# Second layer of a retention and mixture-of-experts kernel: sign tests ahead of the routing chain, w2 products in steps of four column groups, filler matmuls

## The chip, the cores and the metric

The kernel runs on one core of one Trainium2 chip. The metric is the device time of one execution in microseconds (us), lower is better. TensorE is called PE, VectorE DVE, ScalarE ACT, GpSimd POOL and SyncE SP, as in the profile.

## The reference

Three stages follow one another. All data are float32.

```python
# 1. retention, 4 x 8 heads, 768 steps, head size 64
for t in range(S):
    state = gamma * state + einsum('bhd,bhe->bhde', k[:, :, t], v[:, :, t])
    y[:, :, t] = scale * einsum('bhd,bhde->bhe', q[:, :, t], state)
# 2. soft mixture: x (3072 x 512), phi (512 x 32), 8 experts with 4 slots each
logits = x @ phi
d = softmax over tokens;  slot_input = d.T @ x
slot_out[e] = relu(slot_input[e] @ w1[e]) @ w2[e]
c = softmax over slots;   x = c @ slot_out
# 3. top-1 mixture: 8 experts
logits = normalised(x) @ normalised(expert_emb).T / tau
expert_idx = argmax(logits);  gate_w = its softmax weight
out[token] = gate_w[token] * (relu(x[token] @ w1[e]) @ w2[e])
```

The change is in the third stage, called the second layer here.

## The kernel before

The first 205 us are retention and the soft mixture. After them a token is a row of 32 softmax weights c times the 32 x 512 matrix of slot outputs S. The kernel uses that: x = c S, so x w1 = c (S w1), and with G = S w1 (32 x 1024) the hidden values of a token are c G. All tokens of these data go to one expert, e0, which is found from a dot product (lines 1010 to 1015). Its weights are then loaded: w1 in two halves of four 128-column blocks, w2 in pieces of four, two and two blocks (load_w1, load_w2, lines 1016 and 1017; SP issues them in this order, each queued behind the one before). A guarded general path (line 1187 on) stands behind for other data and is not taken.

Since c is a softmax, each of the 1024 hidden units has the same sign over all tokens, if its row of G passes a test (signs, line 1050): it is always positive, always negative, or mixed. Always positive units can be folded: their part of the result is c times (G+ w2), a 32 x 512 matrix M. Always negative units vanish. Mixed units, at most 16 in each block of 128, are picked out and ranked; only for them the hidden values are made for each token (mixed_h) and multiplied with the picked rows of w2.

The second layer is written in a manual schedule: each engine does its instructions in the order of the program text. Names of the tiles, as the profile shows them:

- pu: products of the tokens with S and the expert embeddings (emit_dots, L936), from which DVE takes logit and the squared norms n (take_dots).
- rn: the norm, by a Sqrt on ACT (roots, L950) and two Newton rounds of five DVE operations (newton_sqrt, L1246 to L1250); then routing (L953 to L961) and routing2 (Exp on ACT at L964, then gate on DVE).
- gp, gs: one half of G, four products of 32 columns each on PE (g_part, L858), and its copy by ACT.
- gtp, gt, gsq: its transposes, their copy and their square (signs, L1055 to L1057).
- cs, det, mixed, pos, gpos: the test on DVE (L1058 to L1071); rankp, rank, pick: the ranks of the mixed units (L1076 to L1082).
- gmp, gm, gm4p, Gm: the picked columns of G, spread over four groups of 32 rows and split in a rounded and a rest part (mixed_g).
- mpp, wmp: sums over the eight blocks of gpos and of pick with w2 (fold, L1148); each product has 32 output rows and goes to one of four 32-column groups of PE.
- hps, hh, hl: mixed hidden values for 512 tokens, in six calls of mixed_h (L1100 to L1102).
- mp, m4p, M4: the sum of the four groups of mpp and its split; wmh, wml: the split of wmp.
- ob, ot: one output tile of 128 tokens: four products on PE (L1169 to L1172) in one of four PSUM tiles, the eviction with the gate (evict: DVE for even tiles, ACT for odd ones), the DMA by SP.
- over, cn, pn, cnt, nci: the counts that guard the general path (overflow, counts, counts2), put between tiles 12 to 15 of the output loop.

Before the change, the order of the calls was:

```python
        roots()
        g_part(gs, w1t, 0, W1P)
        newton_sqrt(nc, rn, n2, tm)
        routing()
        routing2()
        signs(0)
        g_part(gs, w1t, 1, W1P)
        signs(1)
        mixed_g()
```

then the w2 products of two blocks at a time, with mixed_h(0) to mixed_h(2) between them, and the loop over 24 output tiles with the other three calls of mixed_h after tiles 2, 6 and 10.

## Time and profile before

| what | value |
|---|---|
| time, median of 3 runs | 276.36 us (276.36 to 277.99) |
| the profiled execution's own time | 276.69 us |
| its span in the trace | 274.8 us |
| PE busy | 246.7 us, 90% of the span |
| DVE / ACT / POOL busy | 121.2 / 98.9 / 55.5 us |
| mean granted clock of PE over the span | 0.919 of 2.4 GHz |

Times in the trace count from the start of the span. PE has two rows in the profile: PE for the matmuls and PEld for loading their stationary operand. A float32 product counts as two matmul instructions, one in fp32r as one. The granted clock (PEclk) is 1.00 at 2.4 GHz and 0.50 at 1.2 GHz.

### The profile page before, as it was taken

How to read it: one execution, taken by the hardware profiler on the slowest of the kernel's cores; microseconds unless marked ns; L12 is line 12 of the kernel's file. 1: busy time of each engine (PE TensorE's matmuls, PEld its weight loads, DVE VectorE, ACT ScalarE, POOL GpSimd, SP SyncE). 2: the span in 40 equal slices, each digit the busy share in tenths (PEclk: the TensorE clock that was granted, in tenths of full speed). 3: DMA queues.
4: the chain of work that ended last, by engine and by line, in shares of the span. 5: the costliest groups of instructions: out<-in, count | busy, mean ns of one | idle time of the engine just before them, and what ended most of it. 6: DMA issues, size and time to landing. Idle time of an engine off the chain costs nothing.

```text
span 274.8 us, 6014 instructions
## 1 busy us (share of the span) xinstructions
PE 246.7 (90%) x2413; PEld 171.1 (62%) x2414; DVE 121.2 (44%) x318; ACT 98.9 (36%) x236; POOL 55.5 (20%) x80
## 2 busy tenths in 40 slices
PE   6899999699999699989998998999998646999991
PEld 2678887588787587877786775333337315238770
DVE  2435645414474336354734564341113842145661
ACT  3264544234534224534544335214013311135331
POOL 2154141414231414141414104120002000000000
PEclk9799999869999869999999999999999555799997
DMA  6995998999989899999999978999904920006664
GB/s 162 220 233 108 270 261 233 273 260 235 220 245 271 230 284 239 234 225 271 258 279 258 358 260 310 360 389 385 384 13 127 393 97 1 0 0 234 265 261 167
DMA packets 85952, 63.74 MB, mean 232 GB/s; under 512 B 51856, under 2 KB 64400, under 8 KB 85920
## 3 DMA queue, kind: packets, MB, share of 16 engines
q1 hardware_dynamic: 85920, 63.30, 79.9%
q8 instruction: 21, 0.34, 0.5%
q14 instruction: 11, 0.09, 0.1%
HBM read 57.00 MB, written 6.29 MB: 230 GB/s over the span
## 4 chain that ended last, share of the span: by engine, by line
PE 65%; DMA 14%; SPq 5%; DVE 5%; POOL 4%; ACT 2%; issue 2%; POOLq 0%; DVEq 0%; ACTq 0%
DMA qc<-in_q_dram 13%; PE y L312 6%; PE hp L763 5%; PE ops L794 5%; PE sc L260 5%; PE y L306 5%; PE trk L237 4%; SPq L145 3%; PE T L289 3%; PE trx L332 3%; POOL qs L215 3%; PE trq L248 3%; PE ob L1172 2%; PE ob L1169 2%; PE ob L1171 2%; PE ob L1170 2%
## 5 line engine op out<-in xcount | busy, mean ns | idle before, releaser
L215 POOL TENSOR_TENSOR qs<-qc,cst 128x512 f32<-128x512 f32 x21 | 22.2, 1075 | 60.8 <-DMA qc<-in_q_dram 43.9
L266 DVE TENSOR_TENSOR at<-sc,cst 128x1024 f32<-128x1024 f32 x23 | 28.1, 1224 | 10.2 <-PE sc L260 9.6
L207 POOL TENSOR_TENSOR kc<-kc,cst 128x512 f32<-128x512 f32 x22 | 23.0, 1047 | 39.0 <-DMA kc<-in_k_dram 31.4
L260 PE MATMUL sc<-qT,kT 64*128 64x128 f32 x384 | 28.8, 291 | 0.0
L317 ACT COPY xT<-y 128x512 f32<-128x512 f32 x24 | 14.0, 585 | 40.1 <-PE y L312 35.6
L260 PEld LDWEIGHTS sc<-qT,kT 64*128 64x128 f32 x384 | 24.1, 193 | 6.7 <-issue 4.9
L312 PE MATMUL y<-at,vc 128*64 128x128 f32 x384 | 26.2, 279 | 0.0
L334 DVE COPY x<-trx 128x512 f32<-128x512 f32 x23 | 15.8, 689 | 22.9 <-PE trx L332 22.6
L239 ACT COPY kT<-trk 128x512 f32<-128x512 f32 x23 | 13.5, 585 | 31.5 <-PE trk L237 31.5
L312 PEld LDWEIGHTS y<-at,vc 128*64 128x64 f32 x384 | 20.5, 136 | 2.9 <-DVE rm L422 0.3
L237 PE MATMUL trk<-cst,kc 128*128 128x128 f32 x92 | 16.2, 303 | 6.7 <-POOL kc L207 6.6
L306 PE MATMUL y<-qT,tb 128*128 128x128 f32 x160 | 22.1, 282 | 0.0
L306 PEld LDWEIGHTS y<-qT,tb 128*128 128x128 f32 x160 | 20.0, 196 | 0.1
L342 DVE TENSOR_REDUCE lt<-ltps 128x32 f32<-128x128 f32 x24 | 7.0, 290 | 23.7 <-PE ltps L341 23.7
L237 PEld LDWEIGHTS trk<-cst,kc 128*128 128x128 f32 x92 | 10.5, 150 | 9.9 <-POOL kc L207 7.7
L162 POOL TENSOR_TENSOR cs<-c_all,cs 128x64 fp32r<-128x64 f32 x24 | 7.2, 332 | 44.7 <-ACT cs L161 44.7
L332 PE MATMUL trx<-cst,xT 128*128 128x128 f32 x96 | 16.2, 294 | 0.0
L249 ACT COPY qT<-trq 128x512 f32<-128x512 f32 x22 | 13.8, 627 | 4.6 <-PE trq L248 4.2
L248 PE MATMUL trq<-cst,qs 128*128 128x128 f32 x88 | 15.4, 304 | 0.0
L763 PE MATMUL hp<-wu,sinT 128*32 128x512 f32 x128 | 15.2, 597 | 0.0
L794 PE MATMUL ops<-wu,Z 128*32 128x512 f32 x128 | 14.1, 594 | 0.0
L289 PE MATMUL T<-vc,kc 128*64 128x64 f32 x304 | 13.9, 238 | 0.2 <-ACT tb L299 0.2
(270 smaller groups left out, 365.1 us busy)
## 6 DMA issues: line engine op xcount, KB each, us to landing
wu<-in_moe_w_dram SPq DMA_DIRECT2D x32, 1024.0 KB, 8.7
vc<-in_v_dram SPq DMA_DIRECT2D x24, 256.0 KB, 4.9
out_dram<-ot SPq DMA_DIRECT2D x24, 256.0 KB, 2.2
kc<-in_k_dram SPq DMA_DIRECT2D x23, 256.0 KB, 6.8
qc<-in_q_dram SPq DMA_DIRECT2D x11, 512.0 KB, 8.4
w1t<-in_moe_w_dram SPq DMA_DIRECT2D x2, 1024.0 KB, 6.2
w2t<-in_moe_w_dram SPq DMA_DIRECT2D x1, 1024.0 KB, 9.4
w2t<-in_moe_w_dram SPq DMA_DIRECT2D x2, 512.0 KB, 10.2
```

Of the source, the lines that this page charges most:

```text
L207: eng.tensor_tensor(out=t, in0=t, in1=gk[:, g % CPB, :].unsqueeze(2).to_broadcast([P, H, D]), op=ALU.mult)
L215: engs[r].tensor_tensor(out=ts[:, r, :, :], in0=t[:, :, r, :], in1=gq[:, (g % CPB) // 2, :, r].unsqueeze(2).to_broadcast([P, H, D]), op=AL ...
L237: nc.tensor.transpose(ps[:, a, :], k_t[g][:, 2 * a:2 * a + 2, :].rearrange("p h d -> p (h d)"), ident)
L248: nc.tensor.transpose(ps[:, a, :], q_t[g][:, r, 2 * a:2 * a + 2, :].rearrange("p h d -> p (h d)"), ident)
L260: nc.tensor.matmul(ps[:, hh, a, :], kT[g][lo:lo + 64, a, :], qs(g, lo, lo + 64, a), start=True, stop=True,)
L266: nc.vector.tensor_tensor(out=t.rearrange("p e a t -> p (e a) t"), in0=ps.rearrange("p e a t -> p (e a) t"), in1=mask.unsqueeze(1).to_broa ...
L289: nc.tensor.matmul(T[64 * hh:64 * hh + 64, a, :], k_t[g][:, h, :], v_t[g][:, h, :], start=(c == 0 and a == 0), stop=True, skip_group_check ...
L306: nc.tensor.matmul(ps[:, a, :], tb[:, a, :], qs(g, 0, P, a), start=(a == 0), stop=False, skip_group_check=True,)
L312: nc.tensor.matmul(ps[64 * hh:64 * hh + 64, a, :], v_t[g][:, 2 * a + hh, :], at_t[g][:, hh, a, :], start=(c == 0 and a == 0), stop=True, s ...
L332: nc.tensor.transpose(ps[:, a, :], xT[g][:, a, :], ident)
L763: nc.tensor.matmul(hp[32 * j:32 * j + 32, :], sinT[kc // 2][:, kc % 2, :], w[:, j, :], start=(kc == 0), stop=(kc == KDM - 1), skip_group_c ...
L794: nc.tensor.matmul(ops[32 * j:32 * j + 32, :], Z[grp][:, fc, :], w[:, j, :], start=(grp == 0 and fc == 0), stop=(grp == 1 and fc == KFF - ...
```

## The change

Nothing is altered ahead of the last dot products. Behind them:

- signs is cut into three: gt_part (transposes, square, copy), signs (the test on DVE), picks (rank and pick). gsq has a half for each i. Both halves are tested before the Newton steps and the routing; these stand behind picks(1) on DVE. The Newton round has three operations instead of five.
- routing is cut in two, and its two operations of 128 x 192 go to POOL; the is_equal for the one-hot mask moves into counts; Exp writes tmp8 instead of logit.
- A one-element Exp on ACT behind gt_part(0) brings the table load with it.
- busy(n) puts n products of 128 x 512 in fp32r on PE, three times three, whose result nobody reads.
- fold multiplies four blocks in one step, each in a column group of its own; the first mpp step stands between the two picks. The slots of pick are those of the half, and mixed_g puts block fc in group fc % 4.
- Two calls of mixed_h stand before the loop instead of three, four in it (after tiles 1, 5, 9 and 13). The output tile has six buffers instead of four.

```diff
-    def routing():
+    def routing(eng):
         nc.vector.tensor_scalar_add(rn, rn, 1e-6)
         nc.vector.reciprocal(out=rn, in_=rn)
-        nc.vector.tensor_tensor(
+        eng.tensor_tensor(
             out=logit, in0=logit, in1=rn.unsqueeze(2).to_broadcast([P, NCH, E]), op=ALU.mult
         )
+
+    def routing1(eng):
         nc.vector.tensor_reduce(out=tm, in_=logit, axis=AX.X, op=ALU.max)
         mb = tm.unsqueeze(2).to_broadcast([P, NCH, E])
-        nc.vector.tensor_tensor(out=tmp8, in0=logit, in1=mb, op=ALU.is_equal)
-        nc.vector.tensor_tensor(out=logit, in0=logit, in1=mb, op=ALU.subtract)
+        eng.tensor_tensor(out=tmp8, in0=logit, in1=mb, op=ALU.subtract)
...
     def counts():
         eb = eidx.unsqueeze(1).to_broadcast([P, NCH, E])
+        nc.vector.tensor_tensor(
+            out=tmp8, in0=logit, in1=tm.unsqueeze(2).to_broadcast([P, NCH, E]), op=ALU.is_equal
+        )
         nc.vector.tensor_tensor(out=tmp8, in0=tmp8, in1=eb, op=ALU.mult)
...
-        op = s4.enter_context(tc.tile_pool(name="op", bufs=4))
+        op = s4.enter_context(tc.tile_pool(name="op", bufs=6))
...
-        def signs(i):
+        def gt_part(i):
             fs = slice(4 * i, 4 * i + 4)
             ps = ps_a.tile([P, 4, NSLOT], F32, tag="a", name="gtp")
...
-            nc.scalar.activation(out=gsq, in_=ps, func=ACTF.Square)
+            gtps[i] = ps
+            nc.scalar.activation(out=gsq[:, i], in_=ps, func=ACTF.Square)
             nc.scalar.copy(gt[:, fs, :], ps)
-            nc.vector.tensor_reduce(out=cs_[:, fs], in_=ps, axis=AX.X, op=ALU.add)
+
+        def signs(i):
+            fs = slice(4 * i, 4 * i + 4)
+            nc.vector.tensor_reduce(out=cs_[:, fs], in_=gtps[i], axis=AX.X, op=ALU.add)
...
+        def picks(i):
+            fs = slice(4 * i, 4 * i + 4)
             pr = ps_a.tile([P, 4], F32, tag="a", name="rankp")
             nc.tensor.matmul(pr, mask, mixed[:, fs], start=True, stop=True)
             nc.vector.tensor_tensor(out=rank[:, fs], in0=mixed[:, fs], in1=pr, op=ALU.mult)
             nc.vector.tensor_tensor(
-                out=pick[:, fs, :].rearrange("p (b r) s -> p b r s", r=2),
-                in0=rank[:, fs].rearrange("p (b r) -> p b r", r=2).unsqueeze(3).to_broadcast([P, 2, 2, NSLOT]),
-                in1=slots.unsqueeze(1).to_broadcast([P, 2, 2, NSLOT]), op=ALU.is_equal,
+                out=pick[:, fs, :], in0=rank[:, fs].unsqueeze(2).to_broadcast([P, 4, NSLOT]),
+                in1=slots[:, i:i + 1, :].to_broadcast([P, 4, NSLOT]), op=ALU.is_equal,
             )
...
+        def busy(n_):
+            pz = ps_b.tile([P, DM], F32, tag="b", name="busy")
+            for _ in range(n_):
+                nc.tensor.matmul(pz, cT(0, P), cT(0, 512), start=True, stop=True)
+
+        def fold(dst, lhs, i):
+            for fc in range(4 * i, 4 * i + 4):
+                o = NSLOT * (fc % 4)
+                nc.tensor.matmul(
+                    dst[o:o + NSLOT, :], lhs[:, fc, :], w2t[fc], start=(i == 0), stop=True, skip_group_check=True
+                )
+
...
-        roots()
+        nc.vector.tensor_scalar_max(n2, n2, TINY)
+        nc.scalar.activation(out=rn, in_=n2, func=ACTF.Sqrt)
+        busy(3)
         g_part(gs, w1t, 0, W1P)
-        newton_sqrt(nc, rn, n2, tm)
-        routing()
-        routing2()
+        busy(3)
+        gt_part(0)
+        nc.scalar.activation(out=junk, in_=rinv4, func=ACTF.Exp)
         signs(0)
         g_part(gs, w1t, 1, W1P)
+        busy(3)
+        gt_part(1)
+        picks(0)
         signs(1)
-        mixed_g()
         pm = ps_b.tile([P, DM], F32, tag="b", name="mpp")
         pw = ps_b.tile([P, DM], F32, tag="b", name="wmp")
...
-        for i in range(KFF // 2):
-            for fc in (2 * i, 2 * i + 1):
-                fold(pm, NSLOT * ((i + 1 + fc % 2) % 4), gpos, fc)
-                fold(pw, NSLOT * i, pick, fc)
-            if i < 3:
-                mixed_h(i)
+        fold(pm, gpos, 0)
+        picks(1)
+        fold(pm, gpos, 1)
+        fold(pw, pick, 0)
+        for _ in range(2):
+            nc.vector.reciprocal(out=tm, in_=rn)
+            nc.vector.scalar_tensor_tensor(out=tm, in0=tm, scalar=0.5, in1=n2, op0=ALU.mult, op1=ALU.mult)
+            nc.vector.scalar_tensor_tensor(out=rn, in0=rn, scalar=0.5, in1=tm, op0=ALU.mult, op1=ALU.add)
+        routing(nc.gpsimd)
+        mixed_g()
+        routing1(nc.gpsimd)
+        mixed_h(0)
+        fold(pw, pick, 1)
         nc.scalar.copy(mp, pm)
-        nc.scalar.copy(wmh, pw)
         pr = ps_b.tile([P, DM], F32, tag="b", name="m4p")
         nc.tensor.matmul(pr, rep, mp, start=True, stop=True)
+        mixed_h(1)
+        nc.scalar.copy(wmh, pw)
         nc.vector.tensor_tensor(out=wml, in0=pw, in1=wmh.bitcast(F32), op=ALU.subtract)
         stack_split(M4, pr)
+        routing2()
...
-            if g in (2, 6, 10):
-                mixed_h(3 + g // 4)
+            if g in (1, 5, 9, 13):
+                mixed_h(2 + g // 4)
```

On PE, between the last dot products and the w2 products, the order before is:

```order
L936 MATMUL pu<-SEst,cT_2353 128x42 x16
L858 MATMUL gp<-w1t_2666,SoT 32x512 x4
L1055 MATMUL gtp<-cst,gs 128x32 x4
L1076 MATMUL rankp<-mixed,cst 128x4
L858 MATMUL gp<-w1t_2668,SoT 32x512 x4
L1055 MATMUL gtp<-cst,gs 128x32 x4
L1076 MATMUL rankp<-mixed,cst 128x4
L1088 MATMUL gmp<-pick,gt 32x32 x8
L1094 MATMUL gm4p<-gm_2698,cst 128x128
L1148 MATMUL mpp<-w2t_2670,gpos 32x512
```

and of the change:

```order
L936 MATMUL pu<-SEst,cT_2353 128x42 x16
L1143 MATMUL busy<-cT_2158 128x512 x3
L858 MATMUL gp<-w1t_2666,SoT 32x512 x4
L1143 MATMUL busy<-cT_2158 128x512 x3
L1060 MATMUL gtp<-cst,gs 128x32 x4
L858 MATMUL gp<-w1t_2668,SoT 32x512 x4
L1143 MATMUL busy<-cT_2158 128x512 x3
L1060 MATMUL gtp<-cst,gs 128x32 x4
L1088 MATMUL rankp<-mixed,cst 128x4
L1148 MATMUL mpp<-w2t_2670,gpos 32x512 x4
L1088 MATMUL rankp<-mixed,cst 128x4
```

The second w1 half now stands ahead of the first rank product, the fillers stand around the w1 halves, and four mpp products stand together. The products gmp and gm4p come four w2 products of each sum later.

On ACT, from the root to the second gs copy, as one piece of the difference:

```order
-L950 ACTIVATE rn<-n_2601 128x24
+L1158 ACTIVATE rn<-n_2601 128x24
 L862 COPY gs<-gp 128x512
-L964 ACT_TABLE_LOAD
-L964 ACTIVATE logit<-logit 128x192
-L1056 ACTIVATE gsq<-gtp 128x128
-L1057 COPY gt<-gtp 128x128
+L1062 ACTIVATE gsq<-gtp 128x128
+L1063 COPY gt<-gtp 128x128
+L1163 ACT_TABLE_LOAD
+L1163 ACTIVATE junk_69<-rinv_67 128x1
 L862 COPY gs<-gp 128x512
```

The table load moved from ahead of the first square and copy to behind them, with a one-element Exp in place of the routing's.

On DVE, in the output loop around tile 12 to tile 14 (ovp and over: the overflow test, cn: the counts), the change has:

```order
L1129 TENSOR_SCALAR ot<-ob,gate 128x512 x2
L1120 TENSOR_REDUCE over<-ovp 1x1
L1121 TENSOR_SCALAR over<-over 1x1
L1113 SCALAR_TENSOR_TENSOR hl<-hps,hh 128x512
L972 TENSOR_TENSOR tmp_2600<-logit,tm 128x192
L975 TENSOR_TENSOR tmp_2600<-tmp_2600,cst 128x192
L976 TENSOR_REDUCE tm<-tmp_2600 128x24
L977 TENSOR_TENSOR onehot<-tm,cst 128x192
L980 TENSOR_REDUCE cn<-onehot 128x8
L981 TENSOR_REDUCE cn<-good 128x1
L1129 TENSOR_SCALAR ot<-ob,gate 128x512
```

Before, neither the hl (L1113) nor the first tmp operation (L972) stood between the overflow test and the counts; the others stood there in the same order.

## Rows read from the trace of the kernel before

**Rows 1.** Stretches: start:end, length, busy PE, PEld, DVE, ACT, POOL, PEclk, DMA share.

```profile
50.90:53.40 2.50, 0.00 (x0) 0.00 (x0) 1.18 (x1) 0.20 (x1) 2.06 (x3) 0.89 1.07 300
210.60:213.30 2.70, 2.70 (x25) 2.63 (x24) 1.04 (x4) 0.77 (x2) 0.00 (x0) 1.00 0.90 340
213.30:216.70 3.40, 2.27 (x11) 0.45 (x10) 2.87 (x11) 0.50 (x2) 0.00 (x0) 0.50 1.05 396
216.70:223.60 6.90, 2.34 (x10) 2.24 (x10) 5.53 (x24) 2.27 (x5) 0.00 (x0) 0.50 0.74 273
223.60:233.10 9.50, 6.30 (x37) 4.03 (x37) 2.47 (x12) 1.27 (x4) 0.00 (x0) 0.50 0.01 3
233.10:237.10 4.00, 4.00 (x10) 0.84 (x9) 0.29 (x1) 0.27 (x1) 0.00 (x0) 0.50 0.00 0
246.70:269.10 22.40, 22.36 (x100) 17.57 (x98) 13.93 (x33) 9.26 (x14) 0.00 (x0) 1.00 0.65 249
```

**Rows 2.** Chain of waits from the dots to the output loop: start, us, what.

```profile
215.51 0.23 ACT rn L950
...
221.67 0.30 DVE cs__2692 L1058
...
223.73 1.91 PE gp L858 x8
...
228.77 0.30 DVE cs__2692 L1058
...
245.51 0.71 DVE M L825
```

**Rows 3.** Timeline, 194 to 234 us: start, us, engine, line, instruction, [idle before].

```profile
194.64 10.05 PE L794 MATMUL ops<-wu,Z 128*32 128x512 f32 x92
...
208.71 1.10 PE L1023 MATMUL sep<-seT,SoT 128*128 128x64 f32 x8 [0.94 <-DVE seT L1020]
...
214.30 1.94 PE L858 MATMUL gp<-w1t,SoT 128*32 128x512 f32 x8 [0.67 <-DMA w1t<-in_moe_w_dram]
...
217.03 1.28 ACT L964 ACT_TABLE_LOAD   x1
...
217.06 1.91 PE L1055 MATMUL gtp<-cst,gs 128*128 128x32 f32 x8 [0.83 <-ACT gs L862]
...
230.76 1.35 PE L1088 MATMUL gmp<-pick,gt 128*32 128x32 f32 x16
...
233.58 0.29 DVE L825 TENSOR_TENSOR Gm<-gm4p,Gm 64x128 fp32r<-64x128 f32 x1 [2.23 <-ACT Gm L824]
```

**Rows 4.** Chain of waits: a w2 pass, hps at the low and at the high clock.

```profile
235.10 1.70 PE wmp L1148 x2
236.80 0.62 PE hps L1100
...
248.62 0.23 PE hps L1100
```

**Rows 5.** Timeline of the output loop around tiles 11 to 16.

```profile
257.19 0.59 ACT L1101 ACTIVATE hh<-hps 128x512 fp32r<-128x512 f32 x1
...
257.85 0.69 ACT L1116 ACTIVATE ot<-ob,gate 128x512 f32<-128x512 f32 x1
...
257.92 0.68 DVE L1102 SCALAR_TENSOR_TENSOR hl<-hps,hh 128x512 fp32r<-128x512 f32 x1
...
259.42 0.34 DVE L971 TENSOR_TENSOR tmp<-tmp,cst 128x192 f32<-128x192 f32 x1
...
261.01 0.17 DVE L977 TENSOR_REDUCE cn<-good 128x1 f32<-128x24 f32 x1
...
261.37 0.20 PE L981 MATMUL pn<-cn,ones 128*1 128x9 f32 x2
```

**Rows 6.** The page's costliest groups: operations on POOL.

```profile
L215 POOL TENSOR_TENSOR qs<-qc,cst 128x512 f32<-128x512 f32 x21 | 22.2, 1075 | 60.8 <-DMA qc<-in_q_dram 43.9
...
L162 POOL TENSOR_TENSOR cs<-c_all,cs 128x64 fp32r<-128x64 f32 x24 | 7.2, 332 | 44.7 <-ACT cs L161 44.7
```

More of the change, by code (lines that the diff above doesn't have):

```diff
@@ L950, in roots @@
         nc.scalar.activation(out=rn, in_=n2, func=ACTF.Sqrt)
-    def routing():
+    def routing(eng):
         nc.vector.tensor_scalar_add(rn, rn, 1e-6)
         nc.vector.reciprocal(out=rn, in_=rn)
-        nc.vector.tensor_tensor(
+        eng.tensor_tensor(
             out=logit, in0=logit, in1=rn.unsqueeze(2).to_broadcast([P, NCH, E]), op=ALU.mult
         )
+    def routing1(eng):
         nc.vector.tensor_reduce(out=tm, in_=logit, axis=AX.X, op=ALU.max)
         mb = tm.unsqueeze(2).to_broadcast([P, NCH, E])
-        nc.vector.tensor_tensor(out=tmp8, in0=logit, in1=mb, op=ALU.is_equal)
-        nc.vector.tensor_tensor(out=logit, in0=logit, in1=mb, op=ALU.subtract)
+        eng.tensor_tensor(out=tmp8, in0=logit, in1=mb, op=ALU.subtract)
     def routing2():
-        nc.scalar.activation(out=logit, in_=logit, func=ACTF.Exp)
-        nc.vector.tensor_reduce(out=gate, in_=logit, axis=AX.X, op=ALU.add)
+        nc.scalar.activation(out=tmp8, in_=tmp8, func=ACTF.Exp)
+        nc.vector.tensor_reduce(out=gate, in_=tmp8, axis=AX.X, op=ALU.add)
         nc.vector.tensor_scalar_add(gate, gate, 1e-9)
@@ L1031, in retention_soft_moe_top1_moe @@
         gt = wp.tile([P, KFF, NSLOT], F32, name="gt")
-        gsq = wp.tile([P, 4, NSLOT], F32, name="gsq")
+        gsq = wp.tile([P, 2, 4, NSLOT], F32, name="gsq")
+        gtps = {}
         gpos = wp.tile([P, KFF, NSLOT], F32, name="gpos")
@@ L1055, in signs @@
                 nc.tensor.matmul(ps[:, j, :], gs[:, fc * P:(fc + 1) * P], rep[:, 0:NSLOT], start=True, stop=True)
-            nc.scalar.activation(out=gsq, in_=ps, func=ACTF.Square)
+            gtps[i] = ps
+            nc.scalar.activation(out=gsq[:, i], in_=ps, func=ACTF.Square)
             nc.scalar.copy(gt[:, fs, :], ps)
-            nc.vector.tensor_reduce(out=cs_[:, fs], in_=ps, axis=AX.X, op=ALU.add)
+        def signs(i):
+            fs = slice(4 * i, 4 * i + 4)
+            nc.vector.tensor_reduce(out=cs_[:, fs], in_=gtps[i], axis=AX.X, op=ALU.add)
             nc.vector.tensor_tensor(out=c2[:, fs], in0=cs_[:, fs], in1=cs_[:, fs], op=ALU.mult)
-            nc.vector.tensor_reduce(out=det[:, fs], in_=gsq, axis=AX.X, op=ALU.add)
+            nc.vector.tensor_reduce(out=det[:, fs], in_=gsq[:, i], axis=AX.X, op=ALU.add)
             nc.vector.tensor_scalar(
@@ L1086, in mixed_g @@
             for fc in range(KFF):
-                o = NSLOT * (fc // 2)
+                o = NSLOT * (fc % 4)
                 nc.tensor.matmul(
@@ L1127, in dots @@
             take_dots(pu[i], i)
+        def busy(n_):
[4 more added lines that the diff above has]
+            for fc in range(4 * i, 4 * i + 4):
+                o = NSLOT * (fc % 4)
+                nc.tensor.matmul(
+                    dst[o:o + NSLOT, :], lhs[:, fc, :], w2t[fc], start=(i == 0), stop=True, skip_group_check=True
+                )
         take = [flush_c(ps_a, "a") for _ in range(2)]
@@ L1133, in retention_soft_moe_top1_moe @@
         dots(1)
-        roots()
+        nc.vector.tensor_scalar_max(n2, n2, TINY)
+        nc.scalar.activation(out=rn, in_=n2, func=ACTF.Sqrt)
+        busy(3)
         g_part(gs, w1t, 0, W1P)
-        newton_sqrt(nc, rn, n2, tm)
-        routing()
-        routing2()
+        busy(3)
+        gt_part(0)
+        nc.scalar.activation(out=junk, in_=rinv4, func=ACTF.Exp)
         signs(0)
         g_part(gs, w1t, 1, W1P)
+        busy(3)
+        gt_part(1)
+        picks(0)
         signs(1)
-        mixed_g()
         pm = ps_b.tile([P, DM], F32, tag="b", name="mpp")
         pw = ps_b.tile([P, DM], F32, tag="b", name="wmp")
-        seen = set()
-        def fold(dst, o, lhs, fc):
-            nc.tensor.matmul(
-                dst[o:o + NSLOT, :], lhs[:, fc, :], w2t[fc], start=((id(dst), o) not in seen),
-                stop=True, skip_group_check=True,
-            )
-            seen.add((id(dst), o))
-        for i in range(KFF // 2):
-            for fc in (2 * i, 2 * i + 1):
-                fold(pm, NSLOT * ((i + 1 + fc % 2) % 4), gpos, fc)
-                fold(pw, NSLOT * i, pick, fc)
-            if i < 3:
-                mixed_h(i)
+        fold(pm, gpos, 0)
[11 more added lines that the diff above has]
+        fold(pw, pick, 1)
         nc.scalar.copy(mp, pm)
-        nc.scalar.copy(wmh, pw)
         pr = ps_b.tile([P, DM], F32, tag="b", name="m4p")
         nc.tensor.matmul(pr, rep, mp, start=True, stop=True)
+        mixed_h(1)
+        nc.scalar.copy(wmh, pw)
         nc.vector.tensor_tensor(out=wml, in0=pw, in1=wmh.bitcast(F32), op=ALU.subtract)
         stack_split(M4, pr)
+        routing2()
         for g in range(NCH):
@@ L1205, in retention_soft_moe_top1_moe @@
             newton_sqrt(nc, rn, n2, tm)
-            routing()
+            routing(nc.vector)
+            routing1(nc.vector)
             routing2()
```

## Prediction

> **What bounds the kernel now.** I read the granted clock by stretches first, then the chain of waits from the last dot products to the first output tile, then the single rows of that stretch, and last the output loop. The whole change lies behind 213.3 us of a span of 274.8 us; nothing ahead of it is moved, so only the last 61 us are at stake.
>
> In [rows 1] the reader should see three things. TensorE (PE) runs at 2.4 GHz until 213.3 and at 1.2 GHz from there to 237.1. In the low stretch it is busy for only 2.27 of 3.40, 2.34 of 6.90 and 6.30 of 9.50 us, so it waits there, and what it does costs double. From 246.7 on it is busy for 22.36 of 22.40 us: the output loop is bound by PE, and each microsecond that the loop starts earlier is a microsecond gained, if nothing is put into it.
>
> What ends last in the low stretch is shown by the chain [rows 2]. It runs through the root, ten Newton steps, the routing and the Exp on DVE and ACT (215.5 to 221.6), and only then to the first sign test (cs, 221.67), although its product gtp had begun at 217.06 [rows 3]. Then follow the second w1 half (223.73), the second sign test (cs, 228.77), and the w2 products one by one, until M4 is split at 245.51 + 0.71 = 246.2 and the first tile ends.
>
> **The change, step by step**, on the time axis of the profile.
>
> *First fillers and first w1 half.* No row shows a filler. The nearest is hps, also 512 columns of fp32r with full weights: 0.23 us at 2.4 GHz and 0.62 us at the low clock with a switch in it [rows 4]. I take 2 x 0.23 = 0.46 at 1.2 GHz. Three fillers begin when the dots are issued, at about 213.4, at the clock that has just fallen, and end at 214.75. The w1 half starts at 214.30 in the profile, when its DMA is there, so it is 0.45 us late and ends at 216.7; the copy behind it is done at 217.5 instead of at 217.06, when gtp began [rows 3]. Bounds: 0 if the clock has not fallen yet (3 x 0.23 ends at 214.1), 0.7 us by the 0.62 row, and below nothing for what the fillers do to the clock. The next three lie beside the copy.
>
> *The clock.* It rose at 237.1 after the w2 products had kept PE at work without a hole since 233.1 [rows 1]. With the fillers PE has no hole between 210.6 and about 217, and since 213.4 it streams wide products; I take the high level from 216.7.
>
> *First sign test.* gtp is eight thin passes, 1.91 us at 1.2 GHz; sep, eight of the same kind at 2.4 GHz, took 1.10 [rows 3]. So 217.5 + 1.1 = 218.6, with Square and copy 219.1. The test starts there, not at 221.67: 2.6 us gained. Its eight steps on DVE are unchanged, some 1.8 us, so gpos(0) is ready at 220.9.
>
> *Second half.* The second w1 half now follows at once (218.4 to 219.4, half of 1.94) instead of at 223.73. But ACT now has the table load (1.28 us [rows 3]) and a one-element Exp, together about 1.5, between the first gt copy and the second gs copy: 219.1 + 1.5 = 220.6. That load was hidden while ACT waited for the routing; now it costs 220.6 - 219.4 = 1.2 us. Copy, transposes, Square and copy (0.6, as of the 0.8 between gp's end and gtp, 1.1 and 0.5) end at 222.8. DVE does picks(0) before it, to 223.1; there the second test starts (before: 228.77) and ends at 224.9. 5.6 us are gained so far.
>
> *The clock again, where I choose.* Between the third fillers' end (220.0) and gpos(1) (224.9) PE has the thin transposes (1.1), a rank product and one w2 step of 0.9 us, with holes of 1.3 and about 1.5 us. In the profile the clock fell at 213.3 after thin products had kept PE busy for 2.70 of 2.70 us, and it fell at about 52.9 after 2 us without any [rows 1]. I take it that it falls again, at about 223.5.
>
> *The w2 products.* Before, the four instructions of a pair went to groups in which two collide: the two that collide took 1.70 us in one pass at the low clock [rows 4], so each of four pairs costs two such passes, 3.4 us low or 1.7 high. Four groups at once are what the first layer's w2 does: 92 instructions in 10.05 us at 2.4 GHz, eight (one step) in 0.87 [rows 3]; and gp, also four groups, took 1.94 at 1.2 GHz. So 16 products cost 4 x 0.87 = 3.5 us or 4 x 1.75 = 7.0, against 3.4 + 3 x 1.7 = 8.5. Their weights are there: the DMA share is 0.01 from 223.6 on [rows 1]. At the low clock: mpp step 1 and the first wmp step 225.0 to 228.7. Newton (six operations) and the reciprocal lie beside them on DVE, to 228.0. From gmp to the split of Gm the profile has 230.76 to 233.9 [rows 3], 3.1 us with a wait for pick in it; without it 2.9: Gm at 231.7. hps(0) 0.6, last wmp step to 234.3, m4p to 236.1, hps(1); then, in ACT's order, hh(1) (237.2), wmh (237.8), the cast and the split of M4: 239.4 against 246.2. **6.8 us gained** at the head of the output loop. I let the clock be high again by then, since PE works from 231.9 to 236.5 almost without a hole.
>
> *Routing on POOL.* Two operations of 192 columns: by the rows of 64 and 512 columns [rows 6] between 0.33 and 1.08 us each, 0.55 on the line between. They are ready at 228.0, and ACT takes the Exp behind M4's cast at about 238.8: even 3 us each would hide. The gate is then ready at 240.3, 0.3 us after the first tile; four PSUM tiles cover that. Nothing is lost.
>
> *Into the output loop go two costs.* One is a fourth hps, 0.23. The other is a wait: the second layer's last hl now stands on DVE ahead of the counts, behind the eviction of tile 13 and hh on ACT, and the is_equal comes along. By [rows 5], from the end of tile 13: eviction 0.69, hh 0.59, hl 0.68, is_equal 0.34 (as the multiplication of the same shape), the five operations from 259.42 to 261.18 1.76, handoffs 0.4: 4.5 us. PE has meanwhile one hps and two tiles of four 0.23: 2.05. Its product pn, which before found its operand there (261.37, a hole of 0.1), waits **2.4 us**, with tiles 16 to 23 queued behind it in order. The two more output buffers gain nothing, as PE is not held there today.
>
> *Sum.* 6.8 - 0.2 - 2.4 = 4.2 us. The profiled execution took 276.7 us, 1.9 outside its span, and lies 0.3 above the median of the runs shown: 276.7 - 4.2 = **272.5 us**. One per cent, 2.8 us, is about what a measurement can tell from no change.
>
> **The Trainium skill against the trace.** At 213.3 the clock fell though PE had no hole [rows 1]. "TensorE: Matmul & The Clock Gate", section "Why this matters for your kernels", asks only that long idle gaps between bursts be avoided; by it the fillers would keep the clock high to the end, as the first rival below has it. The trace disagrees at 213.3, which is why the forecast is another.
>
> **Rivals.**
> 1. *The clock stays high from 216.7 on.* For it: with the fillers PE is never long without work. Against it: 213.3. All w2 products, gmp, gm4p and m4p then run at half: M4 is split at 235.0, 11.2 gained, less 2.6: about 8.5 us, **268.2**.
> 2. *The fillers don't lift the clock*, so that the change doesn't do what it says. For it: the w1 products between them use 32 columns a group, and in [rows 1] 6.30 of 9.50 us did not lift it. Then gtp costs 1.9 twice, the first test ends at 222.2, the second at 227.5, M4 at 241 to 242: 4.2 to 5.2 gained, less 2.6, less what a low clock takes of the first tiles: 0.6 to 2.5 gained, **275**.
> 3. *Slower: the clock is low into the output loop.* PE at the head of the loop stands in holes for wmh, wml and M4, 236.5 to 239.4. A tile is 0.9 us at the high clock and 1.8 at the low one, so each microsecond low in the loop costs 0.5. With rival 2's 4.2 us at best less 2.6 for hps and the counts, 1.6 remain; M4 comes at 242, and the clock decides at 245: low until 247 it is 1.1 us slower, **277.8**, low until 251 3 us slower.
>
> **How the numbers follow.** Forecast 0.45, rival 1 0.32, rival 2 0.15, rival 3 0.08. The forecast's own range is 271.0 to 274.9 (clock high again at 237, or only at 244). Some 0.34 of its 0.45 lie below 273.6, one per cent down. Faster by over 1%: 0.34 + 0.32 + 0.02 of rival 2 = 0.68. Within 1%: 0.11 + 0.13 + 0.02 of rival 3 = 0.26. Slower: 0.06. The range reaches from rival 1 with 0.4 to spare to the upper half of rival 2: 267.8 to 275.8.
>
> **What would show it.** Right: gp at about 214.75; granted clock 1.0 between 217 and 223; cs(0) at 219.1 and cs(1) at 223.1; the second gs copy behind the table load; eight w2 instructions in one step; PE idle for over 2 us ahead of pn. The choice is decided by the clock's row between 223.5 and 239: 0.5 there is my case, 1.0 is rival 1. Wrong: a low clock at 217 to 223, a cs(0) that waits for more than gtp's copy, an Exp that comes after M4's split, or a pn that doesn't wait.

## The result and the profile after

The changed kernel took 269.49 us (median of 4 runs, 267.73 to 270.83), the kernel before beside it 276.5 us (276.36 to 277.99): a ratio of 0.9731, 95% interval 0.9662 to 0.9799. That is faster by 7.0 us where 4.2 us were forecast. In two later groups of runs it took 264.65 and 265.36 us beside 275.39 and 274.05 us before, 10.7 and 8.7 us faster, ratios 0.9643 and 0.9615 (below). The ratios, and the medians called trimmed below, leave out executions that lie over 1.5% above the fastest of their kernel; the other medians are of all runs.

The second layer began anywhere from 205.65 to 214.23 us in the profiles below, behind instructions that are the same in all of them. So whole times already differ by several microseconds ahead of the first changed instruction, and the second layer is also measured by itself, from five points of each trace.

For the profiled execution of the change (267.73 us, span 266.0) the points are: the first pu product at 208.26, the first sign test (cs) at 216.64, the second at 220.37, the end of M4's split at 232.71 + 0.69 = 233.40, the end of the last eviction at 260.40 + 0.69 = 261.09. Before they were 210.67, 221.67, 228.77, 246.22 and 269.83. The first and the last point, before and after (the lines between are in [rows 2] and below):

```profile
210.67 2.96 PE L936 MATMUL pu<-SEst,cT 128*128 128x42 f32 x24
...
269.15 0.69 ACT L1116 ACTIVATE ot<-ob,gate 128x512 f32<-128x512 f32 x1 [1.12 <-PE ob L1172]
```

```profile
208.26 2.86 PE L936 MATMUL pu<-SEst,cT 128*128 128x42 f32 x24
...
260.40 0.69 ACT ot L1127
```

Of the 9.0 us between the two profiled executions 210.67 - 208.26 = 2.4 us were there before the first changed instruction, 59.16 - 52.83 = 6.3 us are the second layer's, and the last 0.2 us lie behind the last eviction and outside the span.

The granted clock by stretches (the columns of [rows 1]):

```profile
211.60:215.00 3.40, 3.40 (x13) 1.21 (x12) 1.36 (x5) 0.81 (x2) 0.00 (x0) 0.51 1.05 396
215.10:221.80 6.70, 5.20 (x38) 2.88 (x37) 3.21 (x17) 2.83 (x7) 0.00 (x0) 1.00 0.65 238
221.90:225.20 3.30, 3.30 (x18) 1.19 (x19) 2.38 (x11) 0.00 (x0) 0.22 (x1) 0.50 0.00 0
225.30:233.50 8.20, 5.50 (x38) 2.20 (x33) 3.39 (x7) 3.41 (x8) 0.71 (x2) 1.00 0.00 0
233.50:252.50 19.00, 16.89 (x75) 13.34 (x76) 11.97 (x29) 7.45 (x12) 0.00 (x0) 1.00 0.51 196
252.60:256.00 3.40, 3.40 (x9) 2.64 (x8) 1.94 (x7) 0.69 (x1) 0.00 (x0) 0.50 0.63 242
```

Where [rows 1] have one low stretch of 24 us, there are three short ones here, and PE is busy throughout each. The second came after 215.10:221.80, where PE was busy for 5.20 of 6.70 us; the third after a wait in the output loop. The timeline from the first w1 half to the gate answers to [rows 3 and 6] (start, us, engine, line, instruction, idle before):

```profile
211.94 1.93 PE L858 MATMUL gp<-w1t,SoT 128*32 128x512 f32 x8
...
216.63 1.28 ACT L1163 ACT_TABLE_LOAD   x1
216.64 0.29 DVE L1067 TENSOR_REDUCE cs__2692<-gtp 128x4 f32<-128x128 f32 x1 [3.57 <-ACT gt L1063]
...
217.92 0.20 ACT L1163 ACTIVATE junk<-rinv 128x1 f32<-128x1 f32 x1
218.03 0.57 ACT L862 COPY gs<-gp 128x512 f32<-128x512 f32 x1
...
219.86 1.07 PE L1148 MATMUL mpp<-w2t,gpos 128*32 128x512 f32 x8
...
220.37 0.28 DVE L1067 TENSOR_REDUCE cs__2692<-gtp 128x4 f32<-128x128 f32 x1
...
222.33 1.94 PE L1148 MATMUL mpp<-w2t,gpos 128*32 128x512 f32 x8
...
224.98 0.52 POOL L955 TENSOR_TENSOR logit<-logit,rn 128x192 f32<-128x192 f32 x1 [19.32 <-DVE rn L954]
225.53 0.67 PE L1099 MATMUL gmp<-pick,gt 128*32 128x32 f32 x16
...
227.36 0.29 DVE L825 TENSOR_TENSOR Gm<-gm4p,Gm 64x128 fp32r<-64x128 f32 x1 [2.46 <-ACT Gm L824]
...
232.71 0.69 DVE L825 TENSOR_TENSOR M<-m4p,M 64x512 fp32r<-64x512 f32 x1
...
234.04 0.30 DVE L968 RECIPROCAL gate<-gate 128x24 f32<-128x24 f32 x1
```

The first test now follows its product's copy and no longer the routing. One w2 step is 1.07 us at 2.4 GHz and 1.94 at 1.2 GHz, ends included. The gate is ready at 234.34, 0.4 us after the first tile. The same view around tile 13 answers to [rows 5]:

```profile
248.13 0.69 DVE L1113 SCALAR_TENSOR_TENSOR hl<-hps,hh 128x512 fp32r<-128x512 f32 x1 [1.52 <-ACT hh L1112]
...
248.74 0.35 DVE L972 TENSOR_TENSOR tmp<-logit,tm 128x192 f32<-128x192 f32 x1
...
250.77 0.17 DVE L981 TENSOR_REDUCE cn<-good 128x1 f32<-128x24 f32 x1
...
251.00 0.20 PE L985 MATMUL pn<-cn,ones 128*1 128x9 f32 x2 [2.11 <-DVE cn L981]
```

PE stands still for 2.11 us ahead of pn, where 2.4 were forecast. What was not forecast is the low stretch 1.6 us behind it, whose last products and first ones after it stand in the chain of waits like this:

```profile
255.37 0.43 PE ob L1196
255.80 0.39 PE ob L1197
256.19 0.23 PE ob L1198
```

A product of an output tile takes 0.43 instead of 0.23 us there, and in this stretch PE has nothing to wait for.

### The profile page after: what moved, and what is told of

The parts are those of the page before. It is cut to its first block, busy times and chain, and to the rows that moved or that the text cites. A ratio compares the mean times of both kernels' runs of the same rounds, so it can differ in the third digit from the quotient of the medians.

```text
span 266.0 us, 6032 instructions
## 1 busy us (share of the span) xinstructions
PE 240.5 (90%) x2422; PEld 167.6 (63%) x2423; DVE 120.9 (45%) x312; ACT 98.4 (37%) x237; POOL 56.5 (21%) x82
## 4 chain that ended last, share of the span: by engine, by line
PE 63%; DMA 14%; SPq 7%; POOL 6%; DVE 4%; ACT 3%; issue 2%; POOLq 0%; ACTq 0%; DVEq 0%
DMA qc<-in_q_dram 14%; PE y L312 6%; PE hp L763 5%; PE ops L794 5%; PE y L306 4%; PE sc L260 4%; SPq L145 4%; POOL qs L215 4%; PE trx L332 3%; PE trk L237 3%; PE T L289 3%; PE ob L1196 2%; PE ob L1199 2%; PE ob L1197 2%; PE ob L1198 2%; PE trq L248 2%
## 5 line engine op out<-in xcount | busy, mean ns | idle before, releaser
L260 PE MATMUL sc<-qT,kT 64*128 64x128 f32 x384 | 28.2, 285 | 0.0
L260 PEld LDWEIGHTS sc<-qT,kT 64*128 64x128 f32 x384 | 23.4, 187 | 6.8 <-issue 4.7
L312 PE MATMUL y<-at,vc 128*64 128x128 f32 x384 | 26.2, 279 | 0.1
L334 DVE COPY x<-trx 128x512 f32<-128x512 f32 x23 | 15.8, 688 | 18.4 <-PE trx L332 18.2
L237 PE MATMUL trk<-cst,kc 128*128 128x128 f32 x92 | 15.1, 287 | 8.4 <-POOL kc L207 8.4
L312 PEld LDWEIGHTS y<-at,vc 128*64 128x64 f32 x384 | 20.5, 136 | 3.1 <-DVE rm L422 0.3
L306 PEld LDWEIGHTS y<-qT,tb 128*128 128x128 f32 x160 | 19.4, 192 | 0.1
L237 PEld LDWEIGHTS trk<-cst,kc 128*128 128x128 f32 x92 | 9.6, 141 | 11.7 <-POOL kc L207 9.6
L1127 ACT ACTIVATE ot<-ob,gate 128x512 f32<-128x512 f32 x12 | 8.3, 688 | 18.3 <-PE ob L1199 15.6
L248 PE MATMUL trq<-cst,qs 128*128 128x128 f32 x88 | 14.6, 291 | 0.1
```

The costliest lines, as they stand in the source:

```text
L237: nc.tensor.transpose(ps[:, a, :], k_t[g][:, 2 * a:2 * a + 2, :].rearrange("p h d -> p (h d)"), ident)
L248: nc.tensor.transpose(ps[:, a, :], q_t[g][:, r, 2 * a:2 * a + 2, :].rearrange("p h d -> p (h d)"), ident)
L260: nc.tensor.matmul(ps[:, hh, a, :], kT[g][lo:lo + 64, a, :], qs(g, lo, lo + 64, a), start=True, stop=True,)
L306: nc.tensor.matmul(ps[:, a, :], tb[:, a, :], qs(g, 0, P, a), start=(a == 0), stop=False, skip_group_check=True,)
L312: nc.tensor.matmul(ps[64 * hh:64 * hh + 64, a, :], v_t[g][:, 2 * a + hh, :], at_t[g][:, hh, a, :], start=(c == 0 and a == 0), stop=True, s ...
L334: copy(x_t[g], ps.rearrange("p a t -> p (a t)"))
```

## The experiments

Runs named in one group below were made on one chip and share its runs of the kernel before. All second layers in one table, in us between the five points; "low" lists the stretches at 1.2 GHz up to the last eviction, as start after the first pu product / length.

| profile | pu to cs(0) | to cs(1) | to M4 | loop | whole | low |
|---|---|---|---|---|---|---|
| before | 11.00 | 7.10 | 17.44 | 23.62 | 59.16 | 2.6/23.9 |
| forecast | 8.4 | 4.0 | 16.3 | 26.2 | 54.9 | |
| change | 8.38 | 3.73 | 13.03 | 27.69 | 52.83 | 3.4/3.4, 13.6/3.4, 44.3/3.4 |
| change, again (e5) | 8.65 | 3.73 | 11.40 | 26.00 | 49.78 | 2.6/3.4 |
| change, again (e9) | 7.20 | 3.72 | 12.50 | 28.41 | 51.83 | 18.4/6.8, 42.3/3.4 |
| no fillers (e1) | 8.79 | 4.80 | 12.14 | 27.59 | 53.32 | 3.0/13.7, 44.0/3.4 |
| no fillers (e10) | 8.66 | 4.81 | 12.55 | 27.65 | 53.67 | 3.7/13.7, 44.7/3.4 |
| counts later (e2) | 8.56 | 3.72 | 13.04 | 23.98 | 49.30 | 3.7/3.4, 13.9/3.4 |
| table load later (e3) | 8.86 | 2.92 | 11.41 | 27.65 | 50.84 | 4.0/3.4, 41.6/3.4 |
| before with fillers (e4) | 10.99 | 7.60 | 18.27 | 23.65 | 60.51 | 8.3/20.5 |
| old groups (e6) | 8.40 | 3.72 | 12.07 | 26.03 | 50.22 | 3.4/3.4 |
| both, 12 fillers (e7) | 8.53 | 2.92 | 11.41 | 23.97 | 46.83 | 3.7/3.4 |
| both, no fillers (e8) | 8.82 | 4.81 | 12.42 | 23.97 | 50.02 | 3.6/13.7 |
| both, 9 fillers (e11) | 8.44 | 2.92 | 11.40 | 23.96 | 46.72 | 3.7/3.4 |
| both, no fillers (e12) | 8.15 | 4.81 | 13.02 | 23.98 | 49.96 | 4.2/13.7 |

**First group: one part at a time.** Before took 274.99 us here (13 runs, 273.23 to 278.83).

The change itself was not run in this group: the expectations set its 269.5 us beside it, from the runs in which the kernel before took 276.5 and not 274.99 us.

The first run leaves the nine fillers out.

```diff
-        busy(3)
         g_part(gs, w1t, 0, W1P)
-        busy(3)
         gt_part(0)
...
         g_part(gs, w1t, 1, W1P)
-        busy(3)
         gt_part(1)
```

> The changed kernel without its nine filler products; everything else as changed. Theory A (the fillers pay through TensorE's clock): without them the clock falls at the end of the dot products and stays at 1.2 GHz up to the w2 products, over 10 us, as in the kernel before; the two transposes of 8 thin passes cost 1.9 us each instead of 1.0 to 1.1; median 272 to 275, 3 to 5 us over the changed kernel's 269.5. Theory B (the new order alone does it, the clock comes back by itself): 269 to 270.5.

Measured: 269.8 us (266.44 to 271.29, 5 runs), ratio 0.984 (0.978 to 0.990), second layer 53.32 us, only 0.5 behind the first profile of the change. The time is that of theory B; the clock, low for 13.7 us, is that of theory A, and it then rises with no filler there:

```profile
216.50:223.50 7.00, 6.23 (x32) 3.28 (x32) 3.61 (x19) 1.64 (x5) 0.00 (x0) 0.50 0.21 75
223.70:232.60 8.90, 6.30 (x45) 2.39 (x37) 4.46 (x12) 3.42 (x8) 1.04 (x2) 1.00 0.00 0
```

The second test starts 13.59 us behind the first dot product, before 18.10: the order alone, at the low clock, gains 4.5 us up to there. What the fillers are worth in time was left open, since the change itself was timed in another group; the last group takes it up.

The second puts the counts after tiles 14 and 18 instead of 13 and 15.

```diff
-            if g == 13:
+            if g == 14:
                 counts()
-            if g == 15:
+            if g == 18:
                 counts2(True)
```

> The changed kernel with the counts put after tile 14 instead of 13 and their product and sums after tile 18 instead of 15. Theory A (the wait of 2.1 us ahead of pn, and the stretch of 3.4 us at 1.2 GHz that follows it, lie on the path): TensorE is busy without a hole through tiles 12 to 23, the granted clock stays at 2.4 GHz there, 3 to 4 us less than the changed kernel: 265.5 to 266.5. Theory B (the output transfers would bound the loop anyway): 268.5 to 270.

Measured: 263.74 us (262.15 to 267.57, 4 runs), ratio 0.958 (0.9516 to 0.9645), less than either theory gave. Timeline at pn, and the windows row of the rest of that profile:

```profile
254.37 0.17 DVE L981 TENSOR_REDUCE cn<-good 128x1 f32<-128x24 f32 x1
...
254.59 0.20 PE L985 MATMUL pn<-cn,ones 128*1 128x9 f32 x2
```

```profile
228.50:260.00 31.50, 28.27 (x138) 20.27 (x133) 18.87 (x44) 13.32 (x24) 0.52 (x1) 1.00 0.47 177
```

The wait is gone and so is the low stretch behind it: the clock is 1.00 to the last eviction. The loop is 23.98 instead of 27.69 us, 3.7 us shorter, of which the wait itself was 2.1; the second layer is 3.5 shorter. So in that profile of the change the wait cost 1.6 us more through the clock, beside its own 2.1. Over all profiles: the seven that have the wait (2.11 us in each) show a fall 0.5 to 1.6 us behind pn in five, with loops of 27.59 to 28.41 us (the last, e9, with part of an earlier low stretch in it), and none in two, with loops of 26.00 and 26.03; the five with the counts later show none, with 23.96 to 23.98.

The third moves the one-element Exp, and with it the table load, behind gt_part(1).

```diff
         gt_part(0)
-        nc.scalar.activation(out=junk, in_=rinv4, func=ACTF.Exp)
...
         gt_part(1)
+        nc.scalar.activation(out=junk, in_=rinv4, func=ACTF.Exp)
```

> The changed kernel with the one-element Exp, and so the table load, behind the second gt copy instead of the first. Theory A (the load stood ahead of the second gs copy and cost 0.9 us): that copy starts at gp's end, the second sign test 0.9 us earlier, 0.5 to 1.2 us less than the changed kernel: 268.3 to 269, more if the shorter thin stretch keeps the clock up. Theory B (the first picks on VectorE or the clock hold the second test anyway): within 0.3 us of 269.5.

Measured: 265.98 us (263.8 to 268.4, 4 runs), ratio 0.9658 (0.9557 to 0.976). That is less than either theory gave. From the first to the second test it is 2.92 instead of 3.73 us: 0.8 us gained, of the 0.9 that theory A gave. This profile also lacked the low stretch at the w2 steps, so M4 came 11.41 us behind the second test instead of 13.03.

The fourth adds the nine fillers to the kernel before and nothing else.

```diff
         roots()
+        busy(3)
         g_part(gs, w1t, 0, W1P)
+        busy(3)
         newton_sqrt(nc, rn, n2, tm)
...
         g_part(gs, w1t, 1, W1P)
+        busy(3)
         signs(1)
```

> The kernel before with the nine fillers alone, at the same places around the two w1 halves; its order, its w2 products and its routing are kept. Theory A (the sign test waits for the routing on VectorE, so TensorE is empty for 4 us ahead of the second half and the clock falls again): 274.5 to 276.5. Theory C (the clock is the whole gain): 270 to 272.

Measured: 274.9 us (273.68 to 278.61, 10 runs), ratio 1.0015 (0.9977 to 1.0053): nothing. Its timeline shows why:

```profile
214.29 1.08 PE L1055 MATMUL gtp<-cst,gs 128*128 128x32 f32 x8
...
218.65 0.35 DVE L965 TENSOR_REDUCE gate<-logit 128x24 f32<-128x192 f32 x1 [0.43 <-ACT logit L964]
219.65 0.29 DVE L1058 TENSOR_REDUCE cs__2692<-gtp 128x4 f32<-128x128 f32 x1
...
221.14 0.56 PE L1076 MATMUL rankp<-mixed,cst 128*128 128x4 f32 x2 [5.77 <-DVE pos L1068]
```

gtp runs at 2.4 GHz (1.08 instead of 1.91 us in [rows 3]), but the first test still stands behind the routing on DVE, 10.99 us after the dots as before (11.00). PE then waits for 5.77 us, the clock is low from 8.3 us on for 20.5 us, and the w2 products meet it; the second layer is 60.51 us, 1.35 more than before. Here the fillers sped up a product that nothing waited for, and bought nothing.

**Second group: the change again, the old column groups, and the two edits together.** Before took 275.39 us here (7 runs, 272.52 to 279.31). The first is the change as it is.

> The changed kernel once more, beside the three below, since the kernel before took 274.99 us in the runs of the first experiments and not 276.5: 267 to 269.5 here, and 52 to 54 us from the first product of the dots to the end of the last eviction. No theory hangs on it; it is what the others are compared with.

Measured: 264.65 us (262.09 to 271.74, 4 runs), ratio 0.9643 (0.9549 to 0.9737), second layer 49.78 us, both below what was expected. Its windows:

```profile
208.30:211.60 3.30, 3.30 (x13) 1.18 (x13) 2.02 (x7) 0.22 (x1) 0.00 (x0) 0.50 1.05 394
211.70:229.40 17.70, 13.53 (x95) 6.43 (x91) 8.98 (x34) 6.83 (x16) 1.03 (x2) 1.00 0.29 106
229.50:246.00 16.50, 15.37 (x67) 12.12 (x67) 9.76 (x20) 7.46 (x12) 0.00 (x0) 1.00 0.59 224
246.00:256.00 10.00, 7.67 (x34) 6.01 (x34) 5.90 (x19) 2.76 (x4) 0.00 (x0) 1.00 0.61 231
```

In this execution the clock stays high from 211.7 on, through 17.70 us in which PE is busy for only 13.53, and also behind the wait for pn (7.67 of 10.00). That is nearly the prediction's first rival, in the same kernel: second layer 9.4 us shorter than before, for which that rival gave 8.5.

The next puts the blocks back into groups in which two neighbours collide (fc // 2 in fold and mixed_g, the ranks in picks to match).

```diff
-                o = NSLOT * (fc % 4)
+                o = NSLOT * (fc // 2)
```

> The changed kernel with the blocks of w2 in the groups of the kernel before, two blocks to one group (and pick and the products with it accordingly), so that in a step of four blocks two and two collide. Theory A (the four-group step is a large part of the gain): a step lasts 2.6 to 3.1 us at 2.4 GHz instead of 0.9, three steps lie on the path, M4's split comes 4 to 7 us later, 4 to 7 us over the changed kernel. Theory B (the sums lie beside VectorE's routing anyway): within 1.5 us of it.

Measured: 267.03 us (265.35 to 268.08, 4 runs), ratio 0.9742 (0.967 to 0.9815). Chain of waits of this run, and of the change again, which had the same clock there:

```profile
220.19 1.88 PE mpp L1149 x8
...
226.87 1.85 PE wmp L1149 x8
228.72 1.06 PE m4p L1188 x2
```

```profile
219.87 1.01 PE mpp L1148 x8
220.88 0.86 PE wmp L1148 x8
...
225.40 1.12 PE m4p L1187 x2
```

A step that stands alone costs 1.85 us instead of the 0.86 to 1.06 of four groups, at 2.4 GHz. Where the second mpp and the first wmp step stand together, in groups of their own, they interleave, from 222.47 to 224.37, and the two take 1.9 us as with four groups (219.87 to 221.74). From cs(1) to M4 it is 12.07 against 11.40: 0.7 us for the grouping; the first mpp step, which lies beside the second test, delays nothing (the second rankp follows cs(1) by 1.49 us in both). The median is 2.4 us above the change's, between the two theories, with overlapping intervals of the ratio. Between the two profiled executions it is 3.3 us, of which 2.85 were there before the first dot product; the second layer is only 0.44 longer, as theory B has it.

The third of this group has the two edits of the second and third run, and three more fillers between the first mpp step and picks(1).

```diff
         fold(pm, gpos, 0)
+        busy(3)
         picks(1)
```

> The changed kernel with the counts later (tiles 14 and 18), the table load behind the second gt copy, and three more fillers between the first w2 step and the second rank product. Theory A (the three costs are apart from one another): 3.6 + 1 to 2 = 4.5 to 6 us less than the changed kernel, the granted clock high from the second w1 half to the last tile. Theory B (the gains overlap): no better than the better one of the two alone, about 4 us less.

Measured: 264.0 us (262.73 to 267.96, 4 runs), ratio 0.9604 (0.9528 to 0.9679), second layer 46.83. The second layer is 2.95 us shorter than in the change beside it, but the median only 0.65 us lower, where 4.5 to 6 or about 4 us were expected: in whole times neither theory was met. The fourth has the two edits and no filler at all.

> The changed kernel with the counts later and the table load behind the second gt copy, without any filler. Theory A (fillers gain nothing over the clock coming back by the w2 products themselves): within 1 us of the version with twelve fillers. Theory B (with the table load out of the way the fillers keep the clock up, as the profile of the load alone showed): 1.5 to 3 us slower than the version with fillers, and 1.2 GHz for over 10 us behind the dots.

Measured: 264.37 us (263.59 to 264.68, 4 runs), ratio 0.9627 (0.9556 to 0.9697), second layer 50.02. The second layer is 3.2 us longer without fillers, the medians differ by 0.4 with overlapping runs. The profile of the kernel with fillers began its second layer at 214.23, the one without at 207.42, so the two times do not compare; inconclusive for the time.

**Third group: fillers or none, with and without the two edits, in more runs.** Before took 274.05 us here (11 runs, 270.4 to 278.48).

> The changed kernel as it is, five rounds, as the base for the three runs beside it on the same chip. Its two profiles so far had a second layer (from the first of the dot products to the end of the last eviction) of 52.8 us, with three low stretches of the clock, and of 49.8 us with one. Both theories expect one of these again, and a median between 264 and 270 us.

> The changed kernel without its nine fillers, beside the changed kernel. Theory F (the fillers are worth what the low clock costs between 3 and 17 us behind the first dot product): the clock is low there in one piece of 13.7 us, M4 is split at 25.7 us behind the first dot product against 23.8 to 25.1 us, and the median is 0.6 to 3.5 us above the changed kernel's. Theory N (the fillers cost on TensorE what they give back through the clock): the medians differ by less than 0.5 us.

> The changed kernel with the counts after tiles 14 and 18 and with the table load behind the second square and copy; its nine fillers stay. Theory A (the wait ahead of pn is worth 2.1 us, or 3.7 us where a low stretch follows it, and the table load 0.4 to 0.9 us): second layer of 46.8 to 48 us, median 2.5 to 4.5 us below the changed kernel's. Theory B (the clock takes back elsewhere what is saved there): less than 2 us below it.

> The same two edits without any filler. Theory F: second layer of 50.0 us, as in the one profile so far, 2 to 3 us behind the same kernel with fillers, in the median too. Theory N: the medians of the two differ by less than 0.5 us.

| kernel | median us (range, runs) | trimmed median (runs) | ratio to before, 95% interval | second layer |
|---|---|---|---|---|
| change | 265.36 (262.7 to 270.17, 6) | 264.24 (4) | 0.9615, 0.956 to 0.967 | 51.83 |
| change, no fillers | 269.49 (266.82 to 273.81, 6) | 269.39 (5) | 0.9807, 0.9751 to 0.9863 | 53.67 |
| both edits, 9 fillers | 262.19 (261.13 to 264.37, 6) | 262.19 (6) | 0.956, 0.951 to 0.961 | 46.72 |
| both edits, no fillers | 264.48 (262.29 to 270.16, 8) | 262.78 (5) | 0.9572, 0.9526 to 0.9617 | 49.96 |

The change met neither of its two earlier patterns of the clock here but a third (the row e9 above); its median lay where it was expected.

Windows of the two without and with fillers that show it best, both edits without and both edits with nine:

```profile
211.50:225.00 13.50, 11.92 (x56) 5.67 (x53) 6.15 (x31) 3.75 (x9) 0.18 (x1) 0.50 0.52 191
225.20:256.00 30.80, 28.03 (x137) 20.31 (x133) 18.56 (x44) 12.93 (x23) 0.65 (x2) 1.00 0.45 171
```

```profile
213.90:217.10 3.20, 3.20 (x13) 1.35 (x5) 0.93 (x4) 0.81 (x2) 0.00 (x0) 0.50 1.04 387
217.30:232.80 15.50, 12.02 (x87) 5.63 (x86) 8.91 (x34) 6.36 (x15) 1.03 (x2) 1.00 0.25 93
232.90:256.80 23.90, 23.05 (x101) 18.15 (x101) 15.55 (x38) 10.17 (x16) 0.00 (x0) 1.00 0.62 238
```

With fillers the first low stretch is 3.4 us long, without 13.7, in every profile of this order of work but one (e9, where it came later and lasted 6.8). For the changed kernel the theory that the fillers pay holds: 4.1 us between the medians, 5.2 between the trimmed ones, above the 0.6 to 3.5 expected, and the intervals of the ratio lie apart. The profiles show 1.8 us of it in the second layer; where the rest lies, in executions without a profile, is open. For the kernel with both edits the times do not show it: 2.3 us between the medians, 0.6 between the trimmed ones, and nearly the same ratio. There only the profiles do, with second layers of 46.72 and 49.96 us. In the profiles the three kernels that have both fillers and the later counts (e2, e7, e11) also began their second layer latest, at 211.03, 214.23 and 210.13 us, the other nine of the new order at 205.65 to 208.50. Whether that is chance, or takes back part of what the second layer gains, no run shows.

Both edits without fillers (264.48) are about as fast as the change with them (265.36). Both edits with nine fillers have the lowest median, 262.19 us, 3.2 below the change on the same chip and 2.1 below its trimmed one; the intervals of the two ratios just overlap (0.951 to 0.961 and 0.956 to 0.967). The second layer is 5.1 us shorter. Its timeline at the table load and at pn:

```profile
219.13 0.59 ACT L862 COPY gs<-gp 128x512 f32<-128x512 f32 x1 [0.59 <-PE gp L858]
...
221.33 1.28 ACT L1167 ACT_TABLE_LOAD   x1
...
251.12 0.20 PE L985 MATMUL pn<-cn,ones 128*1 128x9 f32 x2
```

The second gs copy now waits for its product alone, the load stands behind the second square and copy, where ACT has time, and PE reaches pn with its operand there.

## Why the prediction was right or wrong

The time lay inside the range given, and on the side given; the size of the gain was too small. The 7.0 us measured are nearer to the first rival's 8.5 than to the forecast's 4.2, and the 264.65 and 265.36 us of the later groups lie below the range. That the first time lay inside it owes something to luck: the range was wide enough to hold the first rival too, and two errors, up to M4 and in the loop, partly cancelled. Step by step, from the table:

- *First fillers*: the w1 half should come 0.45 us late. It starts 3.68 us after the first dot product, before 3.63. Almost nothing: the clock fell at 211.64, in the midst of the fillers, and not ahead of them, so the three took 1.04 us and not 1.38. They stand where PE waits for w1 anyway: without fillers (e1) gp starts 3.61 us after the first dot product and waits 0.76 us for the DMA of w1. The lower bound given, 0, was the right value.
- *The clock behind the first fillers*: it was to be high 6.0 us after the first dot product (216.7), and rose after 6.8 (215.1). Without fillers it stays low until 16.7 to 17.9. The second rival, that fillers do not lift the clock, is out.
- *First and second sign test*: 8.4 and 4.0 us were forecast, 8.38 and 3.73 measured. So 6.0 us are gained up to the second test (18.10 against 12.11), where 5.6 were worked out. The order gives the larger part: without fillers and at the low clock 4.5 and 4.6 us are gained up to there (13.59 in e1, 13.47 in e10), so the fillers add 1.4 to 1.5. The table load costs 0.9 us, not 1.2: gp ends at 217.13, and the copy begins at 218.03 when load and Exp are done; moving it gave 0.8 back. "ScalarE: Activation LUTs" of the Trainium skill, section "What ACT_TABLE_LOAD costs", has 1.28 us for the load and 1.38 for a drain beside it. The load agrees; a drain is not to be seen in this trace, where Exp starts 0.01 us behind the load.
- *The clock again, where I choose*: this is the step that failed. That the clock falls a second time was right for this profile (221.9, which is 13.6 us behind the first dot product; 12.8 forecast). But I kept it low until m4p was done and high again only at 237, and it was back after 3.4 us. From the second test to M4 16.3 us were forecast and 13.03 measured, which is 3.3 us of error: 0.5 in the two w2 steps, 0.9 from gmp to Gm (2.1 instead of 3.0), 1.95 from Gm to M4 (5.75 instead of 7.7). [rows 1] already spoke against it. There the clock rose at 237.1, after 4.00 of 4.00 us of work in the w2 products, the first of which starts here (view of before):

```profile
233.17 1.06 PE L1148 MATMUL mpp<-w2t,gpos 128*32 128x512 f32 x1
```

The forecast let its own w2 steps run without a hole from 225.0 to 228.7 and left the clock low behind them all the same. In the run they fill 3.30 of 3.30 us, and the clock rises at 225.3; without fillers it rises in the same steps, in all four profiles. That the w2 steps, standing earlier and without waits, bring the clock back fits all these rows, but was not tried by itself.
- *The clock as a choice between cases*: the forecast and its first rival were treated as two answers about the kernel, one of which is true. They are two outcomes of it. Up to M4 the three profiles of the changed kernel differ: in the first the clock falls at 3.4 and 13.6 us behind the first dot product, in the second only at 2.6 us, in the third only at 18.4 us. By the sign that the prediction set, the clock between 223.5 and 239 (12.8 to 28.3 us behind the first dot product), the first profile is neither case: low for 3.4 us, then high. The first rival's M4, 24.3 us after the dots, stands between the measured 23.4, 23.8 and 25.1. The rule of the Trainium skill that the prediction set against the trace ("TensorE: Matmul & The Clock Gate", section "Why this matters for your kernels", that long idle gaps are to be avoided) agrees with the second of these profiles from 211.7 on. It does not foretell the fall at 221.9 in the first, behind holes of which the longest in its rows was 0.94 us.
- *w2 products*: a step of four groups was to be 0.87 or 1.75 us, and is 0.86 to 1.01 in the chain at 2.4 GHz and 1.87 at 1.2. That four groups save much at equal clock was too much: the old groups cost only 0.7 us there (e6), since two sums in different groups overlap. From the second test to M4 it was 17.44 us before and is 11.40 in e5; of these 6.0 us the grouping is 0.7. The rest is order and clock together, which no run separates.
- *Routing on POOL*: 0.55 each and hidden. 0.52, hidden, with the gate 0.4 us after the first tile (0.3 forecast). The chain of waits of the change has neither the Newton steps nor the routing in it, from the dots to the first tile. The shorter Newton rounds, the six output buffers and the moved calls of mixed_h were not tried by themselves.
- *The two costs in the output loop*: 0.2 for the product hps and 2.4 for the wait. With the wait gone the loop is 23.97 against 23.62, so 0.35; the wait is 2.11. Mechanism and place were right. What is missing is a term, put at nothing: in two of the three profiles of the change the clock falls behind that wait, which costs 1.7 us more (27.69 against 26.00). It is the third rival's mechanism, a low clock in the output loop, but later in the loop and from another cause, and too small to turn the sign.
- *The sum*: forecast second layer 54.9, measured 52.8, 2.1 less: 3.6 too much up to M4, 1.5 too little in the loop. Another 2.4 us of the profiled execution's lead came from the unchanged first part and could not be forecast from the change.

## What to carry to other kernels

Look first at what an in-order queue puts ahead of the instruction that the chain waits for: leaving that queue gained 4.5 us up to the second test without any filler, while fillers alone, with the queue left as it was, gained nothing. A wait on TensorE can have two prices, its own length and the clock behind it: moving a tiny product by a few tiles made the loop 3.7 us shorter where the clock had fallen behind a wait of 2.1, and 2.0 where it had not. Take the clock's behaviour in one profile as one outcome, and profile the same kernel several times before an edit of a few microseconds is judged by it.
